# Loads of 256 positions in 512-byte runs, an unpadded q and 64x64 quadrants for the retention part of a fused kernel

## The chip, the cores and the metric

The kernel runs on one core of a Trainium2 chip. The metric is device time in microseconds (us). All runs of a group are made on the same chip, and each group has its own runs of the kernel before. Their median is 347.39 to 347.64 us in the four groups of experiments, so medians of different groups are compared as they stand. Most executions agree within 0.3%. A ratio is the mean time of one kernel's fast runs over the mean of the fast runs of the kernel before in the same rounds, so it is not quite the ratio of the medians quoted beside it. In the profiles PE is TensorE's matmuls and PEld its weight loads; DVE is VectorE, ACT is ScalarE and POOL is GpSimd.

## The reference

There are 8 batches, 8 heads, 576 positions and 64 elements per head. Retention is attention without softmax: scores are multiplied by a decay that depends on the distance of the positions, and by zero for later positions. Its output becomes 4608 rows of 512 and goes through a feed-forward layer with 2048 hidden units. Abridged:

```python
scores = scale * np.matmul(q, k.transpose(0, 1, 3, 2))
gamma = 1.0 - 2.0 ** (-5.0 - np.arange(H, dtype=np.float32))
Dmat = np.where(rel >= 0, gamma[:, None, None] ** rel[None, :, :], 0.0)
attn_out = np.matmul(scores * Dmat[None, :, :, :], v)
x = np.ascontiguousarray(attn_out.transpose(0, 2, 1, 3)).reshape(B * S, H * D)
h = x @ w_in                                    # 4608x512 @ 512x2048
out = (h * np.clip(h + 3.0, 0.0, 6.0) / 6.0) @ w_out
```

## The kernel before

Retention is computed in pieces. Inside a piece come the scores (`sc`), the decay mask, and scores times v. What lies before the piece is carried by a state (`P`, `X`), a 64x64 matrix for each head, which `O` multiplies with q. The decay is folded into q and v when they are cast to fp16. In the kernel before, a piece is 128 positions and there are 36 of them. q is padded with zeros, so that one matmul can take two heads.

```python
def load(u, eng=None):                 # q, k, v: one position per partition
    # ...
    eng.dma_start(t[p0:p0 + nr], src[b, :, P * c:P * c + nr, :]
                  .rearrange("h s d -> s h d"))      # runs of 64 fp32 = 256 B

def sc(u, hf):
    # ...
    ps = psum.tile([P, 2, 2, P], FP32, tag="ret", bufs=2, ...)   # one PSUM bank
    for i in range(2):
        pr = 2 * hf + i
        for h0 in (0, 64):
            mm(ps[h0:h0 + 64, i], kT[u][:, pr, h0:h0 + 64], qT[u][:, pr], i == 0, True)
    # ... times the mask on VectorE

def pu(u):                             # state
    # ... 8 matmuls k^T v into ps; VectorE: t = ps + X32[b]
    nc.gpsimd.tensor_tensor(out=xn, in0=t, in1=g, op=ALU.mult)   # fp16
    nc.gpsimd.tensor_tensor(out=x3, in0=t, in1=g, op=ALU.mult)   # fp32
```

The feed-forward part works on nine blocks of 512 rows. `up` makes one chunk of 128 hidden units for 512 rows. ScalarE then computes a relu (`u`) and VectorE computes the product that makes the gate (`gt`). The chunk's PSUM buffer is free only after the gate. `down` uses seven products M1 to M7 instead of eight (Strassen-Winograd) in 14 halves per block, with sums in the accumulators `accA` (M1, M6, M7), `accB` (M2, M4) and `accD` (M5, M3).

```python
def up(n, s):
    # ...
    ph = psum.tile([P, 512], FP32, tag="up", bufs=3, ...)        # three buffers
    # ... 8 matmuls
    nc.scalar.activation(ut, ph, ACTF.Relu, bias=cb[:, 0:1], scale=1.0 / 6.0)
    nc.vector.scalar_tensor_tensor(out=gt[n][:, fc, :], in0=ut, scalar=1.0,
                                   in1=ph, op0=ALU.min, op1=ALU.mult)

def down(n, hp):
    # ...
    acc[tag] = psum.tile([P, 2, 256], FP32, tag="acc" + tag, bufs=1, ...)
```

The program allots eight banks of PSUM (a bank is room for 512 fp32 on each partition): 3 for `up`, 2 for `ret` and 3 accumulators. A table of events sets the program order on each engine by slots. A slot is one `up` chunk, one half of a `down` product once `down` has begun (slot 24), and the retention work planned there.

## Time and profile before

The median is 347.33 us (2 runs, 346.61 to 348.04). The profiled execution has a span of 344.8 us.

| part | reading | view |
|---|---|---|
| up to the first `down` matmul | 85.75 us | timeline |
| TensorE busy, 160 to 180 us | 19.90 of 20 us | windows |
| one `up` chunk / one half `down` product | 0.86 / 0.87 us | timeline, start to start |
| retention per 128 positions | 0.43 scores + 0.12 state + 0.45 `O` = 1.0 us | timeline, start to start |
| start of `up` to end of its gate | 2.50 us (156.40 to 158.90) | timeline |

These lines are from the page of the kernel before. The rows with digits cut the span into 40 slices and give the busy share in tenths; PEclk is the granted TensorE clock. The last two lines are groups of instructions: busy us, mean ns of one, and idle time just before.

```profile
PE 297.1 (86%) x4352; PEld 235.8 (68%) x4352; DVE 238.6 (69%) x392; ACT 150.1 (44%) x235; POOL 162.4 (47%) x228
...
PE   3663929776999989999998999999999999999881
...
PEclk9965876989899999999999999999999999999997
DMA  9999999999998599899689979949999801100305
...
DMA packets 166830, 55.72 MB, mean 162 GB/s; under 512 B 158080, under 2 KB 160128, under 8 KB 166784
...
L53 PE MATMUL up<-xt,win 128*64 128x512 f16 x1152 | 154.7, 390 | 2.3 <-DVE gt L283 2.3
...
L283 DVE SCALAR_TENSOR_TENSOR gt<-u,up 128x512 f16<-128x512 f32 x144 | 98.2, 683 | 64.6 <-ACT u L282 64.2
```

The first quarter has a full DMA row and holes in the PE row. Afterwards PE is at 9 nearly everywhere. The `up` matmuls wait for the gate for only 2.3 us in the whole run, so three buffers are enough.

The windows of the same kernel: the stretch and its length, then us busy of PE, PE's weight loads, DVE, ACT and POOL, each with its number of instructions, then granted clock, DMA share (over 1 where packets overlap) and GB/s:

```profile
160.00:180.00 20.00, 19.90 (x314) 16.71 (x312) 16.32 (x25) 9.46 (x16) 13.40 (x17) 1.00 0.76 151
200.00:220.00 20.00, 20.00 (x319) 16.88 (x316) 15.82 (x26) 9.78 (x16) 11.79 (x17) 1.00 0.92 197
```

TensorE is full in both. The timeline of the same kernel, for one chunk: start, duration, engine, line, operation, and in brackets the idle time before it and what ended that:

```profile
156.40 1.06 PE L53 MATMUL up<-xt,win 128*64 128x512 f16 x8
...
157.49 0.69 ACT L282 ACTIVATE u<-up,cb 128x512 f32<-128x512 f32 x1 [0.28 <-PE up L53]
...
158.21 0.69 DVE L283 SCALAR_TENSOR_TENSOR gt<-u,up 128x512 f16<-128x512 f32 x1 [1.05 <-ACT u L282]
```

The gate of a chunk ends 2.50 us after its first matmul. That is longer than the 1.73 us of TensorE work in a slot, so one buffer alone could not keep TensorE busy.

### The profile page before, as it was taken

To read this page: it belongs to the slowest core of one execution; us is meant where nothing else is said; L and a number is where in the kernel's file an instruction comes from. 1 tells how busy PE (TensorE), PEld (TensorE's weight loads), DVE (VectorE), ACT (ScalarE), POOL (GpSimd) and SP (SyncE) were. 2 spreads that over 40 slices of the span, in tenths; PEclk is the share of its full clock that TensorE was granted. 3 is DMA by queue.
4 is the path that set the end of the run, shared out by engine and by line. 5 is a ranking of instruction groups with operands and counts; after the bars stand their busy time and mean duration, and the time that the engine had idled before them with its cause. 6 is when DMAs were issued, how large, how long until landed. Compare 5 with 4: busy or idle time off the path is not lost.

```text
span 344.8 us, 10257 instructions
## 1 busy us (share of the span) xinstructions
PE 297.1 (86%) x4352; PEld 235.8 (68%) x4352; DVE 238.6 (69%) x392; ACT 150.1 (44%) x235; POOL 162.4 (47%) x228
## 2 busy tenths in 40 slices
PE   3663929776999989999998999999999999999881
PEld 1432615444878868888887888878787788777681
DVE  4670635769966984996797599589659956855810
ACT  3341525634354435445443444545553454544320
POOL 5449129736675665666565464355645501001000
PEclk9965876989899999999999999999999999999997
DMA  9999999999998599899689979949999801100305
GB/s 173 229 300 256 225 247 222 205 208 167 198 152 126 131 217 191 198 202 179 102 213 189 197 197 204 180 104 194 151 169 233 124 2 63 63 2 3 124 3 122
DMA packets 166830, 55.72 MB, mean 162 GB/s; under 512 B 158080, under 2 KB 160128, under 8 KB 166784
## 3 DMA queue, kind: packets, MB, share of 16 engines
q1 hardware_dynamic: 164672, 52.97, 78.2%
q0 software_dynamic: 2112, 2.10, 3.6%
q8 instruction: 34, 0.56, 0.8%
q14 instruction: 12, 0.10, 0.1%
HBM read 36.70 MB, written 9.44 MB: 134 GB/s over the span
## 4 chain that ended last, share of the span: by engine, by line
PE 65%; DVE 13%; DMA 9%; POOL 5%; issue 4%; ACT 2%; SPq 1%; DVEq 0%; POOLq 0%
PE up L53 27%; DMA stgk<-in_k_dram 6%; PE sc L53 3%; DMA kT<-k 3%; PE O L53 3%; DVE su L295 2%; DVE at L220 2%; DVE gt L283 2%; PE tp L205 2%; POOL qpad L182 2%; PE accA8M L53 2%; PE accA6M L53 2%; PE accA2M L53 2%; PE accA7M L53 2%; PE accA4M L53 2%
## 5 line engine op out<-in xcount | busy, mean ns | idle before, releaser
L282 ACT ACTIVATE u<-up,cb 128x512 f32<-128x512 f32 x144 | 98.9, 687 | 136.8 <-PE up L53 129.4
L53 PE MATMUL up<-xt,win 128*64 128x512 f16 x1152 | 154.7, 390 | 2.3 <-DVE gt L283 2.3
L283 DVE SCALAR_TENSOR_TENSOR gt<-u,up 128x512 f16<-128x512 f32 x144 | 98.2, 683 | 64.6 <-ACT u L282 64.2
L53 PEld LDWEIGHTS <-win 128*64 128x64 f16 x1152 | 76.4, 113 | 31.7 <-issue 7.8
L53 PEld LDWEIGHTS <-su 128*64 128x64 f16 x1152 | 65.3, 110 | 9.5 <-issue 4.2
L243 POOL TENSOR_TENSOR X<-XT,g 128x256 f16<-128x256 f32 x32 | 29.4, 918 | 89.9 <-DVE XT L242 80.2
L53 PEld LDWEIGHTS <-gt 128*64 128x64 f16 x864 | 49.7, 111 | 11.7 <-issue 7.0
L220 DVE TENSOR_TENSOR at<-sc,maskc 128x512 f16<-128x512 f32 x64 | 41.0, 681 | 5.6 <-PE sc L53 5.6
L184 POOL TENSOR_TENSOR v<-stgv,gv 128x512 f16<-128x512 f32 x36 | 38.4, 1066 | 11.2 <-DMA stgv<-in_v_dram 11.1
L182 POOL TENSOR_TENSOR qpad<-stgq,gq 128x256 f16<-128x256 f32 x64 | 40.8, 658 | 0.0
L53 PE MATMUL sc<-qT,kT 128*64 128x256 f16 x288 | 25.9, 299 | 5.5 <-DMA kT<-k 3.3
L295 DVE TENSOR_TENSOR su<-gt 128x1024 f16<-128x1024 f16 x36 | 29.9, 831 | 0.0
L53 PEld LDWEIGHTS <-kT 128*64 128x64 f16 x288 | 18.5, 118 | 13.4 <-DMA kT<-k 4.6
L205 PE MATMUL tp<-ident,qpad 128*128 128x128 f16 x64 | 8.1, 275 | 22.3 <-POOL qpad L182 12.8
L177 POOL CAST k<-stgk 128x512 f16<-128x512 f32 x32 | 22.0, 688 | 7.4 <-DMA stgk<-in_k_dram 7.4
L205 PEld LDWEIGHTS <-qpad 128*128 128x128 f16 x64 | 5.2, 121 | 25.2 <-POOL qpad L182 13.5
L266 ACT CAST xt<-O 128x512 f16<-128x512 f32 x36 | 20.8, 579 | 3.4 <-PE O L53 3.3
L53 PE MATMUL O<-at,v 128*64 128x128 f16 x288 | 20.2, 225 | 1.0 <-DVE at L220 1.0
L246 POOL TENSOR_TENSOR X<-XT,g 128x256 f32<-128x256 f32 x24 | 19.3, 803 | 0.0
L206 DVE COPY qT<-tp 128x1024 f16<-128x1024 f16 x8 | 5.5, 689 | 16.9 <-PE tp L205 16.9
L53 PEld LDWEIGHTS <-v 128*64 128x64 f16 x288 | 15.8, 114 | 1.7 <-issue 1.4
L53 PE MATMUL O<-qT,X 128*64 128x128 f16 (+1 forms) x256 | 16.4, 213 | 0.0
(149 smaller groups left out, 310.7 us busy)
## 6 DMA issues: line engine op xcount, KB each, us to landing
stgq<-in_q_dram SPq DMA_DIRECT2D x32, 256.0 KB, 4.5
stgk<-in_k_dram SPq DMA_DIRECT2D x32, 256.0 KB, 4.9
stgv<-in_v_dram SPq DMA_DIRECT2D x32, 256.0 KB, 5.2
out_dram<-osb SPq DMA_DIRECT2D x32, 256.0 KB, 3.0
wstg<-in_moe_w_in_dram SPq DMA_DIRECT2D x4, 1024.0 KB, 8.2
wout<-in_moe_w_out_dram POOLq DMA_DIRECT2D x4, 512.0 KB, 12.0
stgq<-in_q_dram SPq DMA_DIRECT2D x8, 128.0 KB, 3.3
stgk<-in_k_dram SPq DMA_DIRECT2D x8, 128.0 KB, 3.3
```

Source lines behind the costliest of these rows:

```text
L53: nc.tensor.matmul(o, l, r, start=start, stop=stop, skip_group_check=True)
L177: ek.tensor_copy(k16[u], stg["k", u])
L182: eq.tensor_tensor(out=qp[:, :, a, 64 * a:64 * a + 64], in0=s[:, :, a, :], in1=bc(ga), op=ALU.mult)
L184: ev.tensor_tensor(out=v16[u], in0=stg["v", u], in1=bc(gv), op=ALU.mult)
L205: nc.tensor.transpose(ps[:, i], src[:, i], ident)
L220: nc.vector.tensor_tensor(out=at[u][:, 2 * hf:2 * hf + 2].rearrange("p c a s -> p (c a) s"), in0=ps.rearrange("p c a s -> p (c a) s"), in1 ...
L243: nc.gpsimd.tensor_tensor(out=xn, in0=t, in1=g, op=ALU.mult)
L246: nc.gpsimd.tensor_tensor(out=x3, in0=t, in1=g, op=ALU.mult)
L266: nc.scalar.copy(xt[n][:, :, P * i:P * i + P], ps)
L282: nc.scalar.activation(ut, ph, ACTF.Relu, bias=cb[:, 0:1], scale=1.0 / 6.0)
L283: nc.vector.scalar_tensor_tensor(out=gt[n][:, fc, :], in0=ut, scalar=1.0, in1=ph, op0=ALU.min, op1=ALU.mult)
L295: e.tensor_tensor(out=o, in0=a, in1=b, op=op)
```

## The change

The change wants longer DMA runs and less padded TensorE work. A piece becomes 256 positions. Two neighbouring positions sit on one partition, so a run is 512 B. q is no longer padded. Scores, state products and inner products become 64x64 tiles, which use all four quadrants of the array. The Trainium skill, "TensorEngine Tiling (Array Packing)", Gotcha 1, says that different row tiles cannot access the same PSUM bank at the same time. The new `ret` tile accordingly has two banks, one for each half of the contraction, and two of them take four banks instead of two. `up` pays with one buffer, and `accB` shares the remaining two with it.

```diff
-            eng.dma_start(t[p0:p0 + nr], src[b, :, P * c:P * c + nr, :]
-                          .rearrange("h s d -> s h d"))           # stg bufs=5
+            SP.dma_start(t.rearrange("p h e d -> p h (e d)"),      # stg bufs=2
+                         src[b, :, P * c:P * c + 256, :]
+                         .rearrange("h (p e) d -> p h (e d)", e=2))
...
+    def ret2(nm):
+        return psum.tile([P, 2, 512], FP32, tag="ret", bufs=2, name=nm)
...          # sc: 16 matmuls 64x64 for two head pairs and 256 positions
+                       kT[w][A, ek, pr, F], qT[w][A, :, pr, F], True, True)
...          # state: copies on ScalarE, arithmetic on GpSimd
+        ACT.copy(sb, ps_P[w])
+        for i in range(2):
...          # src is sb[:, i], or t once there is a state to add
+                POOL.tensor_tensor(out=t, in0=src, in1=X32[b], op=ALU.add)
...
+            POOL.tensor_tensor(out=X32[b], in0=src,
+                               in1=g64 if last and b % 2 == 1 else g128, op=ALU.mult)
+            if i == 0:
+                x16(w, 0)                   # x16(w, 1) follows O
+    def x16(w, i):
+        b = where(w)[0]
+        for a in range(2):
+            A = slice(64 * a, 64 * a + 64)
+            ACT.copy((X16[b] if i else X16[B + w % 2])[A, :, A], X32[b][A])
...          # X16 is block-diagonal now: its zeros are set once, at the start
+        for t in X16:
+            POOL.memset(t[0:64, :, 64:P], 0.0)
+            POOL.memset(t[64:P, :, 0:64], 0.0)
...
-        ph = psum.tile([P, 512], FP32, tag="up", bufs=3, name=f"up{n}_{fc}")
+        ph = psum.tile([P, 512], FP32, tag="up", bufs=2, name=f"up{n}_{fc}")
...
-            acc[tag] = psum.tile([P, 2, 256], FP32, tag="acc" + tag, bufs=1,
+            t = psum.tile([P, 512], FP32, tag="up" if tag == "B" else "acc" + tag,
+                          bufs=2 if tag == "B" else 1, name=f"acc{tag}{n}{m}")
...          # slots of cast, transposes, state+scores, scores, O for each piece
+    TW = {2: (12, 12, 13, 14, 15), 3: (16, 17, 19, 20, 23),
+          4: (17, 19, 22, 26, 30), 5: (20, 22, 27, 31, 37)}
+    for w in range(6, NW):
+        o = 8 * w - 10 + max(0, 12 - w)
+        TW[w] = (o - 19, o - 17, o - 12, o - 8, o)
+    LEAD = 6                                # load: 6 slots before the cast
```

The cast of k moves from GpSimd to ScalarE. In blocks 1 to 4, `up` is cut by halves of the rows, so that it can begin with half a block.

## The prediction

> **What bounds the kernel before.** Until the down projection starts (first accA0M matmul at 85.8 us in the timeline), transfers and latencies: the page's DMA row is at 9 of 10 in nearly every slice, at 170 to 300 GB/s, because 158,080 of 166,830 packets are under 512 B; the 256 B packets of q, k, v take 18 to 24 ns each against 84 ns for 2048 B. Afterwards TensorE: in the windows from 100 to 320 us PE is busy 19 to 20 of 20 us at clock 1.00, and the chain of waits is mostly `up` and `acc` matmuls. The timeline gives 0.87 us for an up chunk, 0.87 us for a half down product, and 0.43 (scores) + 0.12 (state) + 0.45 (inner and cross) = 1.0 us for 128 positions.
>
> **What the change does.**
> 1. Load packets double to 512 B and halve in number. The Trainium skill, DMA: Bandwidth & Descriptors, Specifications, gives 512 B as the least for line rate; the trace's durations suggest (estimate) 27 ns each, some 300 GB/s instead of 217. DMA stops being the limit. But the first two pieces are now a serial chain of 256 positions each, with wide casts and evictions at the cold clock. I estimate the first up at 30 us (before 33.4) and the start of down at 76 us (before 85.8): 10 us gained.
> 2. Unpadded q: scores stream half the columns, 0.44 us per 256 positions instead of 0.87. State has 32 small matmuls instead of 16 (0.24 to 0.48 us); inner and cross stay at 0.88. But 64x64 and 128x64 tiles now alternate. The Trainium skill, TensorEngine Tiling (Array Packing), Key Properties, says that a change of tiling mode drains TensorE; this trace shows 151 ns instead of 55 ns between the last O matmul and the first transpose at 38.7 us, so 0.1 us each, about six per 256 positions. Net 2.2 to 2.4 us against 2.0: perhaps 5 us lost in all.
> 3. A `ret` tile now takes two PSUM banks. `up` pays: two buffers instead of three, shared with accB. In the built order, while M2 and M4 hold one, four successive up chunks wait each for the gate of the one before. Up to gate end is 2.55 us in the trace (156.40 to 158.90, plus release), against 1.74 us of PE work per slot: 0.8 us idle, four times a block, nine blocks: 29 us, of which interleaved scores and O fill perhaps 5. About 24 us lost, all on the critical path.
> 4. State work moves to ScalarE copies and POOL adds. Small.
>
> **Sum.** 347 - 10 + 5 + 24, less some 8 us for fewer late DMA waits (kT transposes, 238 to 262 us) and a share of doubt: 354 us, range 335 to 371. Faster by over 2%: 0.17; within 2%: 0.33; slower by over 2%: 0.50.
>
> **What would show it.** DMA row below 9 early, about 100,000 packets; first accA0M near 76 us (1); `sc` at half the PE time, gaps of 0.1 us at tile changes (2); PE waits of 0.8 us of `up` on DVE `gt`, four per block, and PE at 17 to 18 of 20 us in the middle (3).
>
> **What would make it wrong.** A start much faster than my serial estimate (down starting at 60 us would make it faster overall); freed DMA and POOL removing more late stalls than counted; single-buffer gaps filled by interleaved work; or quadrant matmuls limited by issue, which would make it slower still.

## The result and the profile after

The changed kernel took 395.87 us (2 runs, 395.62 and 396.12), with the result correct. The ratio is 1.1398 (95% interval 1.1292 to 1.1503). It is slower, as was given the largest chance (0.50), but by 48.5 us and not by 7. The time lies far outside the predicted range of 335 to 371 us.

The page of the changed kernel, with the lines that answer to those shown of before, and one new group:

```profile
PE 307.4 (78%) x5664; PEld 251.8 (64%) x5664; DVE 230.2 (58%) x351; ACT 196.3 (50%) x325; POOL 134.5 (34%) x150
...
PE   2336866857899698699969987979698989979980
...
PEclk9999988889999999989998999999999999999997
DMA  8999935998724982893292092807991800400404
...
DMA packets 97783, 52.20 MB, mean 132 GB/s; under 512 B 31680, under 2 KB 93120, under 8 KB 97728
...
L55 PE MATMUL up<-xt,win 128*64 128x256 f16 (+1 forms) x1664 | 158.4, 327 | 42.3 <-DVE gt L322 36.1
...
L276 ACT CAST X<-X 64x256 f16<-64x256 f32 x64 | 25.8, 404 | 26.8 <-POOL X L267 26.4
```

The DMA row is at 8 or 9 in the first five slices still, up to 49 us, and often far lower after that. PE now has holes over the whole run, its `up` matmuls wait 36.1 us for gates, and ScalarE waits 26.4 us for GpSimd in the X copies.

The same two stretches in the windows of the changed kernel, and one from the start of `down`:

```profile
80.00:100.00 20.00, 13.02 (x264) 11.60 (x264) 19.92 (x26) 8.68 (x17) 10.82 (x8) 0.91 1.01 215
160.00:180.00 20.00, 15.53 (x318) 14.15 (x314) 11.40 (x17) 9.10 (x16) 6.67 (x6) 0.91 1.02 221
200.00:220.00 20.00, 15.54 (x317) 14.15 (x315) 8.70 (x15) 9.29 (x18) 3.23 (x4) 0.91 0.57 107
```

PE is at 15.5 of 20 us where it was at 19.9 to 20.0, though no compute engine is saturated there (the first row comes back in section 9). So waits, and not work, are the limit.

The waits of the two kernels (total us, times, longest). First the kernel before:

```profile
PE up L53 <- DVE gt L283: 2.3, 3, 1.6
```

Then the changed kernel:

```profile
PE up L55 <- DVE gt L322: 36.1, 38, 3.7
...
ACT X L276 <- POOL X L267: 26.4, 16, 4.4
...
ACT k L190 <- DMA stgk<-in_k_dram: 8.9, 3, 4.3
...
PE O L55 <- ACT X L276: 8.1, 2, 5.8
```

Of the three waits of the cast of k, two (4.27 and 2.25 us) come at 7 and 12 us, where the kernel before waits too (2.66 and 1.71 us); only the third, of 2.40 us at 282 us, is new.

Two different waits hide in the first line of the changed kernel. I took all pauses of over 0.45 us between two matmul starts from 90 to 380 us: before has 9 of them with 10.5 us in all, after has 36 with 45.9 us. Sixteen of after's are short, 0.84 to 1.01 us, and lie between an `accB` product and the next `up`. Seven are longer than 1.75 us and sum to 19.7 us; five of them end with a gate, two with an output sum on VectorE (`osb`). (Some expectations below say 17 short ones; that was a rougher count.) The timeline of the changed kernel shows one of the long ones:

```profile
199.39 1.04 PE L55 MATMUL up<-xt,win 128*64 128x256 f16 x16
199.52 0.59 ACT L259 COPY Psb<-P 128x512 f32<-128x512 f32 x1
...
200.26 1.04 PE L55 MATMUL accB3M<-wout,gt 128*64 128x256 f16 x16
...
201.00 1.05 POOL L267 TENSOR_TENSOR X<-XT,g 128x256 f32<-128x256 f32 x1
...
202.08 0.82 ACT L276 CAST X<-X 64x256 f16<-64x256 f32 x2 [1.97 <-POOL X L267]
...
202.92 0.58 ACT L421 COPY snap3M<-accA3M 128x512 f32<-128x512 f32 x1
203.53 0.69 ACT L318 ACTIVATE u<-up,cb 128x512 f32<-128x512 f32 x1
204.25 0.69 DVE L322 SCALAR_TENSOR_TENSOR gt<-u,up 128x512 f16<-128x512 f32 x1 [2.79 <-ACT u L318]
...
204.99 1.17 PE L55 MATMUL up<-xt,win 128*64 128x256 f16 x16 [3.69 <-DVE gt L322]
...
205.89 1.97 PE L55 MATMUL accB3M<-wout,gt 128*64 128x256 f16 x16
```

The `up` chunk that starts at 199.39 has its sums ready by 200.4. Its relu stands in ScalarE's queue behind the X cast, which waits for GpSimd until 202.05. So the relu starts at 203.53, the gate ends at 204.94, and PE has stood still for 3.69 us, because the other `up` buffer is held by `accB`. The next product then takes 1.97 us instead of 1.04: the granted clock was halved from 205.8 to 209.2 us. The Trainium skill, "TensorE: Matmul & The Clock Gate", gives an idle window of about 3.4 us for that, under "What's actually happening". After has three such stretches in the middle of the run, before has none from 88.4 to 341 us. Two of the three agree: 3.96 us without a matmul start from 163.8 and from 201.0 us, each followed by 3.4 us at half clock. The third, from 284.3 us, followed pauses of only 1.19 and 2.38 us, and after one of 2.83 us at 128.9 us the clock stayed full, so no single length of pause comes out of this trace.

To see where the time comes from, I read the start of the relu of two `up` chunks in each trace: chunk 24, the first with `down` work beside it, and chunk 143, the last.

```
kernel              chunk 24   chunk 143   between
before                84.3       322.2      237.9
after                 88.9       371.6      282.8
```

4.6 us are lost before `down` begins, and 44.8 us from there to the last chunk.

### The profile page after: what moved, and what is told of

The parts are those of the page before. It is cut to its first block, busy times and chain, and to the rows that moved or that the text cites. A ratio compares the mean times of both kernels' runs of the same rounds, so it can differ in the third digit from the quotient of the medians.

```text
span 394.4 us, 12702 instructions
## 1 busy us (share of the span) xinstructions
PE 307.4 (78%) x5664; PEld 251.8 (64%) x5664; DVE 230.2 (58%) x351; ACT 196.3 (50%) x325; POOL 134.5 (34%) x150
## 4 chain that ended last, share of the span: by engine, by line
PE 50%; DVE 17%; ACT 15%; POOL 6%; issue 5%; DMA 3%; SPq 2%; ACTq 0%; DVEq 0%; POOLq 0%
PE up L55 24%; DVE gt L322 8%; ACT u L318 7%; PE O L55 4%; DVE su L361 3%; DVE tw L153 2%; POOL X L267 2%; ACT k L190 2%; DMA stgv<-in_v_dram 2%; DVE osb L426 2%; DVE at L233 2%; ACT X L276 2%; PE accA8M L55 1%; PE accA7M L55 1%; ACT xt L308 1%
## 5 line engine op out<-in xcount | busy, mean ns | idle before, releaser
L55 PE MATMUL up<-xt,win 128*64 128x256 f16 (+1 forms) x1664 | 158.4, 327 | 42.3 <-DVE gt L322 36.1
L55 PEld LDWEIGHTS <-win 128*64 128x64 f16 x1664 | 101.2, 114 | 71.3 <-issue 52.2
L192 POOL TENSOR_TENSOR v<-stgv,gv 128x1024 f16<-128x1024 f32 x18 | 37.0, 2055 | 33.8 <-PE O L55 21.9
L233 DVE TENSOR_TENSOR at<-sc,maskc 128x512 f16<-128x512 f32 x64 | 40.9, 681 | 11.9 <-PE sc L55 11.7
L264 POOL TENSOR_TENSOR XT<-Psb,X 128x256 f32<-128x256 f32 x24 | 18.9, 786 | 63.4 <-ACT Psb L259 62.1
L276 ACT CAST X<-X 64x256 f16<-64x256 f32 x64 | 25.8, 404 | 26.8 <-POOL X L267 26.4
L192 POOL TENSOR_TENSOR q<-stgq,gq 128x1024 f16<-128x1024 f32 x14 | 28.4, 2030 | 6.1 <-DMA stgq<-in_q_dram 6.1
L190 ACT CAST k<-stgk 128x1024 f16<-128x1024 f32 x18 | 18.7, 1037 | 8.9 <-DMA stgk<-in_k_dram 8.9
L55 PE MATMUL sc<-qT,kT 64*64 64x128 f16 x576 | 15.8, 232 | 2.8 <-ACT kT L212 1.1
L55 PEld LDWEIGHTS <-kT 64*64 64x64 f16 x576 | 10.5, 114 | 6.7 <-issue 4.5
L361 DVE TENSOR_TENSOR su<-su,gt 128x1024 f16<-128x1024 f16 x18 | 14.6, 811 | 0.0
L361 DVE TENSOR_TENSOR su<-gt,su 128x1024 f16<-128x1024 f16 x18 | 14.5, 806 | 0.0
```

The source lines that it names most:

```text
L55: nc.tensor.matmul(o, l, r, start=start, stop=stop, skip_group_check=True)
L190: (e.copy if e is ACT else e.tensor_copy)(o, s)
L192: e.tensor_tensor(out=o, in0=s, in1=bcast(gq if nm == "q" else gv, (2, H), (1, 2), (0, D)), op=ALU.mult)
L233: DVE.tensor_tensor(out=at[w][:, a, 2 * g:2 * g + 2].rearrange("p c k s -> p c (k s)"), in0=ps[:, a].rearrange("p c k s -> p c (k s)"), in ...
L264: POOL.tensor_tensor(out=t, in0=src, in1=X32[b], op=ALU.add)
L276: ACT.copy((X16[b] if i else X16[B + w % 2])[A, :, A], X32[b][A])
```

## The experiments

The theory: after's loss is made of (a) too few `up` buffers while `accB` holds one, (b) casts in ScalarE's queue that wait for GpSimd while relus stand behind them, and (c) a start that is limited by a serial chain, no longer by DMA. Rivals: one cause alone stands for nearly everything; the quadrants are slow on TensorE itself; or 512 B runs do not relieve DMA enough.

### 1. `accB` out of the `up` buffers

`accB` takes the bank of `accD`, which is idle while M2 and M4 are summed.

```diff
-            t = psum.tile([P, 512], FP32, tag="up" if tag == "B" else "acc" + tag,
-                          bufs=2 if tag == "B" else 1, name=f"acc{tag}{n}{m}")
+            t = psum.tile([P, 512], FP32, tag="accA" if tag == "A" else "accD",
+                          bufs=1, name=f"acc{tag}{n}{m}")
```

> Edit: accB goes into the bank of accD (their lives do not overlap), so up has two PSUM buffers to itself. The changed kernel runs 395.9 us, and after 90 us its trace has 36 gaps of over 0.45 us between matmul starts, 45.9 us in all; 17 of them are 0.84 to 1.01 us. Theory A (PSUM: up is left with one buffer while M2 and M4 live): the 0.9 us gaps go, and a second buffer takes most of each long gap too: 30 us or more gained, 361 to 368 us. Theory B (ScalarE stands in line for the state's POOL chain; PSUM only passes it on): the 17 short gaps go (12 us) and the long ones lose about 1 us each: 15 to 20 us gained, 376 to 381 us, with long gaps left. Theory C (tile changes and quadrants cost the time on TensorE itself): under 5 us.

Measured: 381.9 us, ratio 1.1005 (1.0954 to 1.1055). That is 14.0 us less than after. The short pauses from an `accB` product to the next `up` are all gone; six of the long ones stay. Its waits:

```profile
ACT X L276 <- POOL X L267: 26.0, 16, 4.4
...
PE up L55 <- DVE gt L322: 17.5, 17, 3.0
```

So (a) is real, is worth 14.0 us alone, and is not the whole. The gain is below both cases of the expectation: neither A (30 us or more) nor B (15 to 20 us) had the size right.

### 2. The X casts to GpSimd

```diff
-            ACT.copy((X16[b] if i else X16[B + w % 2])[A, :, A], X32[b][A])
+            POOL.tensor_copy((X16[b] if i else X16[B + w % 2])[A, :, A], X32[b][A])
```

> Edit: the fp16 copies of the state (64 of 64x256, 25.8 us of ScalarE, with 26.4 us of waits for POOL ahead of them) are made by POOL, so that nothing in ScalarE's order waits for POOL. PSUM as in the changed kernel. Theory A: the four single-buffer waits per block of 0.9 us stay, about 12 us; the long gaps shrink somewhat: under 10 us gained, 386 us or more. Theory B: the gaps of 1.8 to 4 us go, and the half-clock stretches after them: 20 to 30 us gained, 366 to 376 us, with the 0.9 us gaps left. Theory C: under 5 us.

Measured: 384.0 us, ratio 1.1035 (1.1003 to 1.1066): 11.9 us less than after. Now the long pauses go (two over 1.75 us remain, 4.9 us in all), and 19 short ones are there. The gain lies between the two cases expected (under 10, 20 to 30 us). GpSimd is busy for 163.1 us here instead of 134.5.

```profile
PE up L55 <- DVE gt L322: 26.8, 36, 3.0
```

The edit also takes 25.8 us of busy time from ScalarE. That busy time was not the limit: ScalarE was at 9.3 of 20 us from 200 to 220 us, where PE stood still. The trace points to the order in the queue; no run moves the order alone and leaves the work on ScalarE.

### 3. Both

> Both edits. If A and B are separate causes of the same waits, nearly all gaps after 90 us go: 35 to 45 us gained, 351 to 361 us; the rest over the kernel before (347) is then start (4.6 us later at the 24th up) and tile changes (0.3 us per 256 positions, 4 to 5 us). If it gains no more than the better of the two alone, they are one cause. Theory C: 380 us or more.

Measured: 366.25 us, ratio 1.0529 (1.0501 to 1.0557): 29.6 us less than after. The two edits give 14.0 + 11.9 = 25.9 apart, so 3.7 us come only when both are made. A reason that would fit, not tested: the spare buffer can hide a late relu, and a punctual relu frees the buffer earlier. The gain is more than either alone, so there are two causes, but it stays under the 35 to 45 us expected.

```profile
PE up L55 <- DVE gt L322: 8.7, 8, 4.4
```

19 pauses with 21.8 us remain of 36 with 45.9. The time from chunk 24 to chunk 143 falls to 250.4 us; chunk 24 itself stays at 88.7.

### 4. The zeros of X later

At the start, GpSimd sets the zeros of ten X tiles before it does anything for the second piece. In the timeline of the changed kernel, the last of 20 clears, the cast of v that had to wait for them, the product of the state, and the first matmul that needed it:

```profile
19.21 0.31 POOL L116 MEMSET X<- 64x256 f16 x1
19.60 1.90 POOL L192 TENSOR_TENSOR v<-stgv,gv 128x1024 f16<-128x1024 f32 x1
21.46 0.73 POOL L267 TENSOR_TENSOR X<-Psb,g 128x256 f32<-128x256 f32 x1
...
22.68 1.06 PE L55 MATMUL O<-qT,X 128*64 128x128 f16 x8 [5.83 <-ACT X L276]
```

The clears run from 12.7 to 19.5 us, and PE then waits for 5.83 us. The edit clears only the tiles that are needed at once and the others later:

```diff
-        for t in X16:
+    def clear_x16(ts):
+        for t in ts:
...
     build_state_consts()
+    clear_x16(X16[B:])
...
     state(0)
+    clear_x16(X16[:2])
...
     ou(1)
+    clear_x16(X16[2:B])
```

> Edit: at the start POOL clears only the two state tiles needed first before it casts v of the second piece; the other sixteen clears come later. In the changed kernel POOL clears from 12.7 to 19.5 us, the v cast and the first state product wait behind it (state ready 22.2 us), and PE idles 5.8 us there. If POOL's order sets the start: 4 to 6 us gained, 390 to 392 us, and the first up starts near 29 us instead of 34.7. If the loads of pieces 0 and 1 or the w_in casts set it: under 2 us.

Measured: 392.02 us, ratio 1.1272 (1.1246 to 1.1298): 3.9 us less than after, just under the expected 4 to 6. Chunk 24 moves from 88.9 to 84.5 us, and the first `up` from 34.7 to 31.2 and not to 29. The same edit on top of both mends of experiment 3 (run `e6_both_zero_late`):

> The changed kernel with all three mends: accB in the bank of accD, state copies on POOL, late clears. If they add up: 366.25 - 3.9 = 362.4 us, within 2 us. If the time gained at the start is lost in waits later: 365 us or more.

Measured: 362.59 us, ratio 1.0452 (1.0405 to 1.05): 3.7 us less than experiment 3.

### 5. The kernel before with long runs

This tests what DMA relief alone is worth. The kernel before loads q, k and v as if eight heads of a position lay together, in runs of 2048 B. It moves as many bytes at the same points of the program, but the wrong data; the result is wrong (relative error 1.415).

```diff
-                eng.dma_start(t[p0:p0 + nr], src[b, :, P * c:P * c + nr, :]
-                              .rearrange("h s d -> s h d"))
+                rows = src[b].rearrange("h s d -> (h s) d")
+                eng.dma_start(t[p0:p0 + nr].rearrange("p h d -> p (h d)"),
+                              rows[H * P * c:H * (P * c + nr), :]
+                              .rearrange("(p r) d -> p (r d)", r=H))
```

> The kernel before, with one edit that gives a wrong result on purpose: q, k and v are loaded as 2048 B runs (the same bytes, from other rows) instead of 256 B runs, so that a load takes half the DMA time or less. Theory S (the kernel before starts slowly because its loads saturate the DMA engines, as the prediction says): the 24th up chunk comes at 74 us or earlier instead of 84.3, and the time falls by 8 us or more, to 339 or less. Rival T (casts, transposes, evictions and their order set the start; the DMA engines are busy but not waited for): under 3 us, 344 or more. In between: both.

Measured: 336.05 us, ratio 0.9688 (0.9655 to 0.9722): 11.3 us less than the kernel before. Chunk 24 starts at 73.5 instead of 84.3 us, and from there to the last chunk nothing changes (238.0 against 237.9). From its page:

```profile
DMA  7999998864563993897499389459968601100305
...
DMA packets 70062, 55.72 MB, mean 167 GB/s; under 512 B 47488, under 2 KB 49536, under 8 KB 70016
```

So the transfers did hold up the start of the kernel before, by about 11 us, and its schedule could use the relief. To relieve DMA was a sound intent. The changed kernel relieved DMA too (its row falls to 3 of 10 at about 50 us), but its start became later: experiments 4 and 6 show the gain lost to the clears and to a table that brings the third piece (`TW[2]`) only in slot 12; that wide casts one after the other took a part is not shown. Runs of 512 B relieve less than the 2048 B of this experiment, about as I had put down: where one size of packet runs alone, the windows give 218 GB/s for 256 B (before, 4 to 14 us), 293 GB/s for 512 B (after, 4 to 12 us; my estimate was 300) and 394 GB/s for 2048 B (here, 8 to 16 us). What 512 B alone would give the kernel before was not run; 11 us is for 2048 B.

### 6. Earlier pieces at the start

This is experiment 4 on both mends, with pieces 2 to 5 three to ten slots earlier (the expectation says 6 to 10), the clears in slot 7, and `up` of block 0 taking the accumulators' banks too, which are idle then.

```diff
+        tag = ("up", "accA", "up", "accD")[s % 4] if n == 0 else "up"
...
-    TW = {2: (12, 12, 13, 14, 15), 3: (16, 17, 19, 20, 23),
-          4: (17, 19, 22, 26, 30), 5: (20, 22, 27, 31, 37)}
+    TW = {2: (2, 5, 7, 8, 10), 3: (7, 10, 13, 14, 16),
+          4: (11, 13, 17, 19, 22), 5: (17, 19, 23, 27, 31)}
...
+    at_t(7, lambda: clear_x16(X16[:B]), 4)
+    at_t(0, lambda: load(3), 0)
...          # q of pieces 2 and 3 cast on GpSimd; wsum four slots earlier
```

> As e6, and pieces 2 to 5 are cast, transposed and used 6 to 10 slots earlier, while TensorE waits for gates anyway, and the first sixteen up chunks take turns in four PSUM banks (two of them the idle accumulators). In the changed kernel the first 12 slots take 1.28 us each because of two buffers, and slots 12 to 17 take some 20 us because piece 2 is cast, transposed and used in one go. If these serial stretches set the start: the 24th up comes near 74 us instead of 88.9, 346 to 354 us in all. If something else limits the start (loads, VectorE at 19.9 of 20 us busy from 80 to 100 us): 358 us or more.

Measured: 354.72 us, ratio 1.0226 (1.018 to 1.0272), an interval on both sides of 2%, so the verdict is unclear. It is 7.9 us less than the run before it in this chain. Chunk 24 starts at 77.0 us instead of 85.3: all of the gain lies in the start. Both figures fall just short of the expectation (346 to 354 us, 74 us). The edit has several parts, and which of them counts is not told apart.

### 7. Loads and casts earlier in the rest

What remained in that trace were pauses such as one of 2.16 us at 248.5 us, where the cast of k on ScalarE had waited 3.93 us for its load. So casts go 3 slots earlier, transposes 2 and loads 5 (run `e9_lead`):

```diff
-        TW[w] = (o - 19, o - 17, o - 12, o - 8, o)
-    LEAD = 6
+        TW[w] = (o - 22, o - 19, o - 12, o - 8, o)
+    LEAD = 8
```

> As e8 but the cast of k stays on ScalarE: the earlier loads alone. If it is the late load that matters and not the engine: equal to e8 within 1.5 us. If the position in ScalarE's order matters: 3 us or more slower than e8.

Measured: 348.72 us, ratio 1.0031 (1.0008 to 1.0053): the same as the kernel before, and 6.0 us less than experiment 6. Neither case of the expectation came: it is 8.5 us faster than e8, which follows below. From chunk 24 to chunk 143 it takes 242.0 us instead of 250.4; chunk 24 itself comes later, at 80.8 us. Its waits:

```profile
PE up L55 <- DVE gt L324: 6.3, 5, 2.8
```

The waits for gates are nearly gone. From its page:

```profile
PE   2447885849699999999999999999999999999880
...
PEclk9999999699999999999999999999999999999997
DMA  8999999998182896992699179959314002200404
```

PE is at 9 from the twelfth slice nearly to the end, and the clock is full from 66.1 to 342.6 us.

A variant also moved the cast of k from ScalarE to GpSimd (run `e8_lead_k_pool`), to take the last foreign wait from ScalarE's queue:

```diff
-            at_t(c_, lambda w=w: (cast1(w, "q", POOL), cast1(w, "k", ACT),
+            at_t(c_, lambda w=w: (cast1(w, "k", POOL), cast1(w, "q", POOL),
```

> As e7, and from piece 4 on the cast of k is made by POOL, and for pieces 6 to 17 loads, casts and transposes come 2 to 5 slots earlier. In e7 ScalarE still waits for the load of k once for 3.9 us (246.1 us) with the gates behind it, and TensorE waits 2.1 us for kT (237 us). If waits in ScalarE's order are what is left of the loss: 5 to 9 us gained over e7's 354.7, 346 to 350 us. If VectorE (19 of 20 us busy at 70 to 90 us) or tile changes hold the rest: under 3 us.

It missed: 357.19 us, the median of three fast runs (354.81 to 359.16; a fourth, of 360.79, slow), ratio of the fast ones 1.0271 (1.0208 to 1.0333). That is 8.5 us worse than without it. GpSimd, which has the state too, is busy for 186.8 us instead of 168.5; chunk 24 comes 5.4 us later, at 86.2 us, and the way to chunk 143 takes 246.5 us instead of 242.0. GpSimd was not free to take more.

### 8. The price of the quadrants

All score matmuls are done twice, on experiment 3, which adds 576 quadrant matmuls without a further change of tile mode.

```diff
-        for i in range(2):
+        for i in (0, 1, 0, 1):
```

> e3 (366.25 us) with each score matmul issued twice, right result: 576 more 64x64 matmuls of 128 columns. In the trace of the changed kernel sixteen of them take 0.22 us (0.32 to 0.35 to the next group, with the tile change). If quadrants run four at a time as that says: 18 x 2 x 0.22 = 8 us at most, some of it in waits: 370 to 374 us, so that all quadrant scores together are worth 8 us and Theory C can't explain a loss of 48. If they cost more than the trace shows: 378 us or more.

Measured: 372.0 us, ratio 1.0697 (1.0668 to 1.0726): 5.75 us above experiment 3. So the rival that quadrants are slow on TensorE falls: doing all scores once more costs under 6 us of 372. For state and `O` the trace has to do. From matmul starts in the trace of after, 256 positions take 0.27 (state) + 0.67 (scores) + 1.14 (`O`) us, with the changes of tile inside and behind them, plus about 0.2 for the two changes ahead of them: 2.31 us in all, against 2.0 before. Over 18 pieces that is some 4 to 6 us.

The stage as the timeline of the changed kernel shows it:

```profile
214.40 0.64 PE L55 MATMUL O<-qT,X 128*64 128x128 f16 x16
214.97 0.64 PE L55 MATMUL O<-at,v 64*64 64x128 f16 x32
215.54 1.06 PE L55 MATMUL accA3M<-tw,su 128*64 128x256 f16 x16
...
218.18 1.04 PE L55 MATMUL up<-xt,win 128*64 128x256 f16 x16
219.15 0.45 PE L55 MATMUL P<-v,k 64*64 64x64 f16 x32
219.43 0.40 PE L55 MATMUL sc<-qT,kT 64*64 64x128 f16 x16
```

From the `up` at 218.18 to the state matmuls it is 0.97 us and not 0.87: a change of tile mode costs 0.10 us here, and 0.12 to 0.13 at the other edges of the stage. The Trainium skill, "TensorEngine Tiling (Array Packing)", Key Properties, says that a change of mode drains TensorE. The trace agrees as far as it goes: it shows a pause at each change, and its size.

### 9. Two attempts to pass the kernel before

The clears spread over slots 24 to 38, on `e9_lead` (run `e11_clear_spread`), and then the differences of w_out three slots earlier (run `e12_wsum_early`):

```diff
-    at_t(7, lambda: clear_x16(X16[:B]), 4)
+    for i in range(B):
+        at_t(24 + 2 * i, lambda i=i: clear_x16(X16[i:i + 1]), 4)
```

```diff
-        at_t(DSTART - 10 + 2 * i, lambda i=i: wsum(i, 0, 4, DVE), 4)
-        at_t(DSTART - 9 + 2 * i, lambda i=i: wsum(i, 4, 8, DVE), 4)
+        at_t(DSTART - 13 + 2 * i, lambda i=i: wsum(i, 0, 4, DVE), 4)
+        at_t(DSTART - 12 + 2 * i, lambda i=i: wsum(i, 4, 8, DVE), 4)
```

> As e9 (348.7 us), and the sixteen late clears of state tiles, which stand ahead of the casts of piece 3 and 4 in POOL's order at 48 to 54 us, are spread over slots 24 to 38. In e9 TensorE waits 3.9 us for the state copy at 57 to 61 us. If that wait is POOL's order alone: 2 to 4 us gained, 344.5 to 346.5 us, just under the kernel before. If VectorE sets the pace there: under 1 us.

> As e11, and the eight weight sums on VectorE come three slots earlier, before the casts on POOL that stretch them from 0.7 to 2.4 us each. If VectorE holds back the start of the down projection: 2 to 5 us more, 340 to 344 us, faster than the kernel before by over 1%. If w_out has not landed by then, TensorE waits longer: slower than e11.

Measured: 347.43 us (6 runs), ratio 0.9996 (0.9958 to 1.0034), and 348.88 us (6 runs), ratio 1.0034 (1.0003 to 1.0064). Both are the same as the kernel before. The first gained 1.3 us, between its two cases; the second is a miss. The idea behind it was that VectorE, near its limit at the start of `down`, sets the pace there. In the trace of after VectorE is busy for 19.92 of 20 us from 80 to 100 us, and the same kind of subtraction takes 0.68 us at one time and 2.38 at another:

```profile
74.31 0.68 DVE L153 TENSOR_TENSOR tw<-wout 128x1024 f16<-128x1024 f16 x1
...
80.30 2.38 DVE L153 TENSOR_TENSOR tw<-wout,tw 128x1024 f16<-128x1024 f16 x1
```

GpSimd was casting during the long one. The Trainium skill, "SBUF — State Buffer", Who interferes with whom, says that a VectorE instruction with two SBUF inputs contends with a GpSimd instruction that reads SBUF. That fits, but another such subtraction, at 76.70 us, also took 0.68 us though GpSimd began a product at 76.76. No run isolates it, and `e12_wsum_early` gave nothing. So the contention is argued and not shown to set the time.

## Why the prediction was wrong

The direction was right (slower by over 2% had a chance of 0.50), and two mechanisms were; but the forecast of slower rested on the buffers and tiles alone, and those make at most half of the loss (14.0 to 17.8 and 4 to 6 us of 48.5). The size was wrong: 48.5 us and not 7. The steps, one by one:

- **"State work moves to ScalarE copies and POOL adds. Small."** This step failed. I weighed the busy time of the copies (25.8 us in all, on an engine at half load) and not their place. An X cast waits for a chain on GpSimd, and every relu behind it waits too (26.4 us of waits in the page). Moving it away gave 11.9 us alone, and 15.7 with `accB` out of the way (381.9 to 366.25). The Trainium skill, "PSUM — Partial Sum Buffer", Engine vs sequencer instructions, says that ScalarE's queue is strict FIFO. The trace agrees: relu at 203.53, ready since about 200.4. I had the order of the instructions and did not follow one chain through it.
- **"10 us gained" at the start.** This step failed as well. `down` began at 88.6 us, not at 76, and the first `up` at 34.7, not 30. I had written that it is a serial chain, but counted neither the clears on GpSimd (3.9 us, experiment 4) nor the slots of the table (7.9 us, experiment 6). That relieved DMA can be worth 11 us is true (experiment 5, with runs of 2048 B), but only to a schedule that uses it.
- **"less some 8 us for fewer late DMA waits (kT transposes, 238 to 262 us)".** This step failed in its sign, and there was next to nothing to save: in the trace of before TensorE is busy for 27.8 of 28 us from 236 to 264 us, and after 90 us its matmuls wait 0.3 us for kT. The change added such waits instead: after 90 us, 9.1 us on GpSimd and 2.4 us on ScalarE before casts of q, v and k. Loads now start 6 slots before their cast instead of 10, with two buffers of 256 positions instead of five of 128. In the run of experiment 7 none of these waits is left after 90 us, and it gave back 6.0 us. That edit moved loads, casts and transposes together; which of them counts more is not told apart.
- **"About 24 us lost, all on the critical path" for the `up` buffers.** The mechanism was right and the term mis-sized: 14.0 us alone, 17.8 with the casts moved (384.0 to 366.25). The pause of 0.8 us came as predicted (0.84 to 1.01), but only 16 times and not 36: scores and `O` between two chunks fill more of them than the 5 us that I had allowed.
- **Quadrants and tile changes, "perhaps 5 us".** Right: 2.31 us per 256 positions, inside the predicted 2.2 to 2.4, about 4 to 6 us in all. There was some luck in it: the state takes 0.27 us and not 0.48, and the six changes 0.10 to 0.13 us each and not 0.1, and these two misses partly cancel.
- **"about 100,000 packets".** Right: 97,783. So was the rate of 512 B packets: 293 GB/s for the estimated 300.

Adding up the measured mends: 29.6 (both edits) + 3.7 (clears) + 7.9 (start) + 6.0 (loads and casts) = 47.2 us, which takes the changed kernel from 395.9 to 348.7. These steps bring the loss back. They do not restore the kernel before: chunk 24 comes 3.5 us earlier than there (80.8 against 84.3), the way to chunk 143 takes 4.1 us longer (242.0 against 237.9), and the rest 1.6 us longer (24.1 against 22.5). What keeps the mended kernel from the 336.05 us of experiment 5 can be read from the chunks: it is 7.3 us later at chunk 24 (80.8 against 73.5), 4.0 us slower from there to chunk 143 (242.0 against 238.0), and 1.9 us slower behind it. The second agrees with the cost of the tiles. The third is found in every run with `accB` in the bank of `accD` (24.1 to 25.4 us behind chunk 143, against 22.8 in after and in experiments 2 and 4), so that mend has a price of its own at the end. What limits the start between 60 and 95 us stays open.

No version beats the kernel before. The best, `e11_clear_spread`, equals it.

## What to carry to other kernels

When a change takes PSUM buffers, compare the time from first matmul to release (here 2.5 us) with the work per slot (1.73 us) at the worst moment, and then look at what else stands in the queue of the engine that frees the buffer: an instruction there that waits for a slower engine's chain costs its wait, not its duration. Relieving a saturated resource pays only if the schedule behind it is moved forward too. Before a layout change is judged, mend what it disturbed, one cause at a time: here five mends, two of them bundles of edits, turned 14% slower into the same time.

## What the Trainium skill lacked or had wrong

- "TensorEngine Tiling (Array Packing)" says that a change of mode drains TensorE, but gives no price: 0.10 to 0.13 us each here (0.97 against 0.87 us from an `up` chunk to state matmuls).
- "DMA: Bandwidth & Descriptors", Specifications, gives 512 B as the least transfer for line rate. Here 512 B packets moved 293 GB/s (after, 4 to 12 us) and 2048 B packets 394 GB/s (experiment 5, 8 to 16 us), so 512 B was not yet at the rate of longer runs.
- "TensorE: Matmul & The Clock Gate" states, under "Wait — 56ns, not 53.3ns?", that matmuls start no closer than about 25 ns apart, and does not except small tiles. For 64x64 quadrants it is less: 32 state matmuls of 64 columns took 0.274 us (8.6 ns each), so the quadrants run side by side.
- The same page gives an idle window of about 3.4 us for the halved clock. In experiment 3 the clock was halved at 253.5 us after one pause of 2.16 us between matmul starts.
- No page that I used has a number for what an in-order engine loses the others when it holds a waiting copy ahead of PSUM evictions: 11.9 us here, of 396.
- "SBUF — State Buffer" has no number for an fp16 subtraction of 128x1024 on VectorE beside a GpSimd cast: 0.68 us alone and 2.38 us beside it here, by the trace and not by an experiment.
